# A gated feed-forward behind a chunked scan, one core: seven block products of eight for half of the tiles of blocks 2 and 3 too

## The chip, the cores and the metric

One core of a Trainium2 chip runs the whole kernel. The engines are TensorE (PE), VectorE (DVE), ScalarE (ACT), GpSimd (POOL) and SyncE (SP, which here issues most DMAs). Each engine works through its own list of instructions in order and waits on semaphores. The metric is the device time of one execution in microseconds (us).

## The reference

The first part is a linear attention in chunks over x [4, 8, 768, 32] with decay a and B, C of state size 16; its output, as rows of 256 values per token, goes through a gated feed-forward:

```python
attn_out = _attn_ref(x, a, B, C)                       # [4, 8, 768, 32], a scan over the sequence
x = attn_out.transpose(0, 2, 1, 3).reshape(3072, 256)  # tokens x d_model
gate = 1.0 / (1.0 + np.exp(-(x @ w_gate)))             # w_gate, w_val: 256 x 1536
val = x @ w_val
return gate * val @ w_out                              # w_out: 1536 x 256
```

## The kernel before

The sequence is cut into six chunks of 128 positions; with 4 batches a chunk is a block of 512 tokens, and the blocks are numbered 0 to 5. For each block the scan leaves the feed-forward's input, and then come 12 f tiles of 128 columns of w_gate and w_val.

Everything is fp32, and TensorE's operands are split into a high and a low part (xh, xl; the two halves of w; of h). A product of fp32 values is three matmuls: high by high, high by low, low by high. A gate or value tile of one block (`products_of`, L1244) sums over two halves of d_model, so it is 2 x 3 matmuls of 128x512. ACT takes the sigmoid out of the PSUM bank (L1184), DVE multiplies by the value bank (L1205), ACT writes the high part of h (L1209) and POOL or DVE the low part (L1211). The projection by w_out follows when a block's 12 tiles are done: `proj_turned` (L1529) for blocks 1 to 3, two accumulators of 128x512 over 12 tiles of three matmuls each. DVE turns these back into rows (L1536), and SP stores them with 16 DMAs per block (L1543).

Blocks 4 and 5 are worked as one, "joined". A pair of f tiles, a pair of blocks and the two halves of d_model make a product of 2x2 blocks by 2x2 blocks, and that is done with seven block products in place of eight. The seven stationary operands of an f pair are four blocks of w itself or sums of them (`s_block` builds the sums: one add of high and low parts, L1323, four adds of 128x128, L1330, a high part, L1333, a low part, L1335), and the moving operands are inputs or sums of inputs (`x_block`: x-b11, b21, b22, t1 to t4). `group(i)` issues the seven products, 3 matmuls each (L1368), into three PSUM banks a, b and d (`gva`, `gvb`, `gvd`); even i is a gate, odd i the value of the same f pair. `corner(i, n)` takes the four results 11, 22, 21, 12 out: ACT copies one bank (L1401), DVE adds the other (L1403), then a sigmoid (L1406) or a product with the gate (L1410). Each copy or add frees a bank that the next product needs. `h_parts` makes the two parts of h (L1420, L1422), and `out_of` adds its share to the accumulators of the outputs (matmuls of 256 columns, L1455, so that blocks 4 and 5 come out in rows). `stored_rows` and `last_rows` (L1469, L1479, L1481) copy these and store them.

The scan runs beside all this, in pairs of units named chunk_batch (4_0, 4_2, 5_0, 5_2). Its matmuls stand in `block(n)`: block7, for instance, needs the weighted masks m of units 5_0 and 5_1 (`weights`, L777 on DVE), block8 those of 5_2 and 5_3.

The order of the work is a table, ORDER (from L18). Each word of it, such as pe.group3 or dve.corner3_11, sends one step of a named task to an engine; an engine's instructions stand in the order of its words. Where a step may run on two engines, the table's prefix decides. Tiles in SBUF are shared over time by tags ("h0" to "h11", "r0", "ab", ...): a tile that takes a tag over waits for the readers of the one before.

Of the kernel before, what the change touches and what calls it, by code (L numbers as in the profile page):

```python
# [95 lines left out]
pool.value2_6 pe.block6 dve.value2_7 dve.decays5_3 act.value2_7 pool.value2_7 pe.gate2_8 dve.result4_0
act.inner4_2 sp.x5_2 dve.result4_0 pool.before5_0 dve.after4_2 pe.value2_8 dve.after4_2 act.gate2_8
dve.after4_2 dve.after4_2 pool.decays5_2 pe.gate2_9 dve.value2_8 pool.decays5_3 dve.after4_2 act.value2_8
dve.after4_2 pe.value2_9 act.gate2_9 pool.value2_8 dve.weights5_0 sp.p5_2 dve.weights5_0 pe.gate2_10
dve.value2_9 dve.turn5_2 act.value2_9 pe.value2_10 act.gate2_10 pool.value2_9 act.turn5_2 pe.gate2_11  # L100
# [1777 lines left out]
```

## Time and profile before

| | before |
|---|---|
| median of 3 runs (lowest, highest) | 352.55 us (351.44, 353.85) |
| the profiled execution, and its span | 352.14 us, 350.4 us |
| PE, DVE, ACT, POOL busy | 343.4, 231.2, 174.6, 170.9 us |
| DMA, mean over the span | 78 GB/s |

A span runs from the first to the last instruction. Busy times of different engines overlap; which of them sets the end is read from the chain of work. Starts and ends of matmuls are modelled, and the time of an instruction includes what it loses to others once it has begun.

### The profile page before, as it was taken

How to read it: one execution, taken by the hardware profiler on the slowest of the kernel's cores; microseconds unless marked ns; L12 is line 12 of the kernel's file. 1: busy time of each engine (PE TensorE's matmuls, PEld its weight loads, DVE VectorE, ACT ScalarE, POOL GpSimd, SP SyncE). 2: the span in 40 equal slices, each digit the busy share in tenths (PEclk: the TensorE clock that was granted, in tenths of full speed). 3: DMA queues.
4: the chain of work that ended last, by engine and by line, in shares of the span. 5: the costliest groups of instructions: out<-in, count | busy, mean ns of one | idle time of the engine just before them, and what ended most of it. 6: DMA issues, size and time to landing. Idle time of an engine off the chain costs nothing.

```text
span 350.4 us, 8223 instructions
## 1 busy us (share of the span) xinstructions
PE 343.4 (98%) x3306; PEld 275.9 (79%) x3306; DVE 231.2 (66%) x406; ACT 174.6 (50%) x328; POOL 170.9 (49%) x179
## 2 busy tenths in 40 slices
PE   8989999999999999999999999999999999999995
PEld 4568477787788888888878788888888888888884
DVE  7878678777597687684653336357767677574553
ACT  2565874425965531244551235553546574654542
POOL 6536676666779763235646656866001516032100
PEclk9999999999999999999999999999999999999999
DMA  7998974335646635634300011000002000000003
GB/s 172 209 273 221 278 242 124 110 82 88 137 123 141 134 73 112 115 70 91 61 20 4 2 30 32 0 0 2 1 0 59 4 0 2 0 0 2 0 2 120
DMA packets 87419, 27.43 MB, mean 78 GB/s; under 512 B 75670, under 2 KB 80214, under 8 KB 87382
## 3 DMA queue, kind: packets, MB, share of 16 engines
q1 hardware_dynamic: 82806, 26.13, 31.4%
q10 hardware_dynamic: 4576, 0.79, 1.2%
q8 instruction: 26, 0.43, 0.5%
q14 instruction: 11, 0.09, 0.1%
HBM read 23.46 MB, written 3.44 MB: 77 GB/s over the span
## 4 chain that ended last, share of the span: by engine, by line
PE 86%; DMA 2%; DVE 2%; ACT 1%; POOL 1%; SPq 1%; issue 0%; POOLq 0%; DVEq 0%; ACTq 0%
PE pg L1244 16%; PE pv L1244 16%; PE po L1529 14%; PE acc L1455 8%; PE po L1568 7%; PE gva L1368 6%; PE gvb L1368 6%; PE gvd L1368 5%; DMA wr<-in_moe_w_val_dram 2%; PE banks L784 2%; PE banks L768 1%; PE banks L814 1%; PE acce L1449 1%; POOL w L496 1%; PE acc L1449 1%; DVE wr L459 1%
## 5 line engine op out<-in xcount | busy, mean ns | idle before, releaser
L1211 POOL TENSOR_TENSOR h<-g,h 128x512 fp32r<-128x512 f32 x35 | 47.4, 1355 | 34.8 <-ACT h L1209 34.7
L1244 PE MATMUL pg<-xh,w 128*128 128x512 f32 x168 | 59.3, 394 | 0.0
L1244 PE MATMUL pv<-xh,w 128*128 128x512 f32 x168 | 58.9, 391 | 0.1
L1529 PE MATMUL po<-h,w 128*128 128x512 f32 x216 | 51.3, 392 | 0.0
L1529 PEld LDWEIGHTS po<-h,w 128*128 128x128 f32 x216 | 40.2, 188 | 8.6
L1205 DVE TENSOR_TENSOR g<-pv,g 128x512 f32<-128x512 f32 x36 | 24.8, 689 | 33.3 <-PE pv L1244 33.2
L1209 ACT CAST h<-g 128x512 fp32r<-128x512 f32 x34 | 21.1, 620 | 34.9 <-DVE g L1205 33.3
L1244 PEld LDWEIGHTS pg<-xh,w 128*128 128x128 f32 x168 | 31.5, 188 | 7.8 <-DVE h L1201 0.8
L1244 PEld LDWEIGHTS pv<-xh,w 128*128 128x128 f32 x168 | 31.5, 188 | 7.2 <-POOL w L496 0.5
L1244 PE MATMUL pg<-xl,w 128*128 128x512 f32 x84 | 32.7, 390 | 0.0
L1244 PE MATMUL pv<-xl,w 128*128 128x512 f32 x84 | 32.7, 389 | 0.0
L1184 ACT ACTIVATE g<-pg 128x512 f32<-128x512 f32 x44 | 26.3, 598 | 12.5 <-PE pg L1244 12.2
L1455 PEld LDWEIGHTS acc<-w,h 128*128 128x128 f32 x219 | 29.8, 189 | 2.3
L1455 PE MATMUL acc<-w,h 128*128 128x256 f32 x219 | 30.6, 282 | 0.0
L496 POOL TENSOR_TENSOR w<-wr,w 128x512 fp32r<-128x512 f32 x18 | 26.7, 1483 | 7.7 <-ACT w L494 6.8
L574 DVE TENSOR_TENSOR_SCAN ab<-ab,delta 128x512 f32<-128x512 f32 x20 | 26.7, 1353 | 2.8 <-DMA ab<-a_z 2.8
L1422 POOL TENSOR_TENSOR h<-c,h 128x512 fp32r<-128x512 f32 x7 | 11.4, 1645 | 34.9 <-ACT h L1420 34.9
L477 POOL TENSOR_TENSOR wr<-wr 128x512 int32<-128x512 int32 x18 | 19.9, 1113 | 12.5 <-ACT wr L475 7.7
L1568 PE MATMUL po<-wr,h 128*128 128x256 f32 x96 | 23.4, 394 | 0.1
L1420 ACT CAST h<-c 128x512 fp32r<-128x512 f32 x24 | 14.7, 622 | 15.9 <-DVE c L1410 11.8
L1403 DVE TENSOR_TENSOR c<-gva,c 128x512 f32<-128x512 f32 x12 | 8.3, 691 | 21.1 <-PE gva L1368 21.1
L1568 PEld LDWEIGHTS po<-wr,h 128*128 128x128 f32 x96 | 17.6, 188 | 4.3 <-DVE h L1201 0.5
(205 smaller groups left out, 690.1 us busy)
## 6 DMA issues: line engine op xcount, KB each, us to landing
ab<-a_z SPq DMA_DIRECT2D x40, 128.0 KB
wr<-in_moe_w_gate_dram SPq DMA_DIRECT2D x6, 512.0 KB
wr<-in_moe_w_val_dram SPq DMA_DIRECT2D x6, 512.0 KB
wr<-in_moe_w_out_dram SPq DMA_DIRECT2D x6, 512.0 KB
xn<-in_x_dram SPq DMA_DIRECT2D x10, 256.0 KB
out_dram<-o SPq DMA_DIRECT2D x48, 32.0 KB
bn<-in_B_dram SPq DMA_DIRECT2D x10, 128.0 KB
tn<-in_B_dram SPq DMA_DIRECT2D x32, 32.0 KB
```

The lines of the kernel that those rows point to most:

```text
L477: nc.gpsimd.tensor_tensor(out=lw.bitcast(I32), in0=hw.bitcast(I32), in1=lw.bitcast(I32), op=ALU.add)
L496: engines[eng].tensor_tensor(out=lo, in0=lw, in1=hi.bitcast(F32), op=ALU.subtract)
L574: nc.vector.tensor_tensor_scan(out=t.rearrange("p h l -> p (h l)"), data0=t.rearrange("p h l -> p (h l)"), data1=delta.rearrange("p h l -> ...
L1184: nc.scalar.activation(gs[k, f], pm, AF.Sigmoid)
L1205: nc.vector.tensor_tensor(out=g, in0=pm, in1=g, op=ALU.mult)
L1209: copies[eng](hh, g)
L1211: engines[eng].tensor_tensor(out=hl, in0=g, in1=hh.bitcast(F32), op=ALU.subtract)
L1244: nc.tensor.matmul(pm, w[:, part, kt, fs], xx[:, kt], start=(i == 0), stop=(i == 3 * NK - 1))
L1368: nc.tensor.matmul(out, one, two, start=m == 0 and n in (1, 7, 2), stop=m == 2, skip_group_check=True)
L1455: nc.tensor.matmul(mine, one(js), w[:, two, :], start=first and m == 0 and (k == 0 or alone), stop=final and m == 2, skip_group_check=True,)
L1529: nc.tensor.matmul(acc, w[:, part], hs[k, f][:, of_h], start=f == starts[0] and i == 0, stop=f == starts[-1] + size - 1 and i == 2,)
L1568: nc.tensor.matmul(acc[:, :DM], hs[k, f][:, js], whole[NF + f // 2][:, f % 2], start=start, stop=stop, skip_group_check=True,)
```

## The change

Blocks 2 and 3 become a first joined pair for f tiles 6 to 11 (`PAIRS`). Their tiles 0 to 5 are computed as before, and `tiles(k)` ends their plain loop there. The joined work is now 18 groups: q0 to q5 are the three f pairs 6 to 11 of blocks 2 and 3, q6 to q11 the same f pairs of blocks 4 and 5, and q12 to q17 f pairs 0 to 5 of blocks 4 and 5 (`tile_of`, `stage`). The sums of w for the f pairs of q0 to q5 are used again by q6 to q11.

The moving operands of the first stage are the inputs xh, xl of blocks 2 and 3 themselves and four sums made of them (`x_early`, x0t1 to x0t4); those of the second are x1b and x1t. The projection of blocks 2 and 3 is no longer one run of matmuls: `out_early` adds tiles 0 to 5 and `out_of` the shares of the first stage, into four accumulators of 128x512 that stay until `turned_rows` turns and stores both blocks in groups q7 to q9. Sums of w are built in the order 6 to 11, then 0 to 5, in two tiles that are used for all of them (`kept_tile`).

ORDER is laid out anew from the first tiles of block 2 on, about 145 us into the span. Its core in the diff:

```diff
-pe.gate2_4 dve.value2_3 sp.p4_2 dve.after4_0 act.value2_3 dve.after4_0 pe.value2_4 dve.after4_0 sp.x5_0
-pool.value2_11 pe.proj2_0 dve.result4_2 act.inner5_0 pool.before5_2 dve.result4_2 dve.after5_0 pool.xt3_0
+dve.before5_0 pe.outa3_0 pe.outa3_1 dve.result4_2 dve.result4_2 pool.before5_2 dve.weights5_2 pe.outa3_0
+pe.block9 pe.outa2_0 pe.outa2_0 pe.outa2_0 pool.s6 dve.s6 pool.s7 dve.result5_2 dve.result5_2 pe.group0 act.s6
...
     def value(k, f):
-        eng = yield step(("act", "dve"), (ACT_SB, DVE_1), [("proj", k - 1)] + held)
-        hs[k, f] = hp.tile([P, 2, 512], F32R, tag=f"h{f}", name=f"h{k}_{f}")
+        eng = yield step(("act", "dve"), (ACT_SB, DVE_1), [("proj", min(k, 2) - 1)] + held)
+        place_of = f + 6 * (k == NCH - 3)
+        hs[k, f] = hp.tile([P, 2, 512], F32R, tag=f"h{place_of}", name=f"h{k}_{f}")
...
+    def tiles(k):
+        return NF if k < NCH - 4 else NF // 2
...
-    T1, T2 = NCH - 1, NCH - 2
+    PAIRS = ((NCH - 3, NCH - 4), (NCH - 1, NCH - 2))
+    T1, T2 = PAIRS[1]
+    NS, NQ7 = 9, 18
...
+    def tile_of(q):
+        return q + 6 if q < 6 else q if q < NF else q - NF
...
+    def x_early(name):
...
+        eng = yield step(("dve", "pool"), (DVE_MM, 1.29), needs + xs(k2) + (xs(k1) if name != "t3" else []), made, port=True)
+        in0, in1 = first()
+        t = kept_tile(to)
+        engines[eng].tensor_tensor(out=t, in0=in0, in1=in1, op=ALU.subtract)
+        for n, (k, part, m, op) in enumerate(more):
+            eng = yield step(("dve", "pool"), (DVE_MM, 1.29), [], [("t0", name)] if n == len(more) - 1 else [], port=True)
+            engines[eng].tensor_tensor(out=t, in0=t, in1=of(k, part, m), op=op)
+        yield step("act", ACT_SB, home)
+        hi = x_part(0, name, 0)
+        nc.scalar.copy(hi, t)
+        eng = yield step(("dve", "pool"), (DVE_MM, 1.29), [], [("x7", 0, name, 0)], port=True)
+        engines[eng].tensor_tensor(out=x_part(0, name, 1), in0=t, in1=hi.bitcast(F32), op=ALU.subtract)
...
-    def group(i):
+    def group(q):
+        i, at, last = tile_of(q), stage(q), q - 1
...
+    def h_parts(s, n):
...
+        elif s == 4:
+            needs = [("stored", k2)] if m == 3 else [("hused", 2, PLACES[m + 1])]
...
+    def turned_products(block, mt, f, h, first, final):
+        w = wo[f // 2][:, f % 2, :, mt * P : (mt + 1) * P]
+        for m, (one, two) in enumerate(((0, 0), (0, 1), (1, 0))):
+            nc.tensor.matmul(
+                acc_of(block, mt), w[:, one], h[:, two], start=first and m == 0, stop=final and m == 2, skip_group_check=True
+            )
+
+    def out_early(k, mt):
+        fs = [2, 3, 4, 5, 0, 1] if k == PAIRS[0][0] else list(range(6))
+        for f in fs:
...
+            yield step("pe", 3 * 0.227, needs, [("outa", k, mt, f)], port=12)
+            turned_products(k, mt, f, hs[k, f], f == fs[0], False)
...
+    def out_of(s, n):
...
+        if s < 3:
+            for mt in range(2):
+                yield step("pe", 3 * 0.228, [("h7", s, n), ("w", NF + f // 2), ("outa", block, mt, 1)], ([("hused", s, n)] if mt else []) + [("o7", s, n, mt)], port=12)
+                turned_products(block, mt, f, hj[s, n], False, (s, n) == (2, last))
+            return
...
+    def turned_rows(k):
+        last = "21" if k == PAIRS[0][0] else "12"
+        for mt in range(2):
+            yield step("dve", 0.74, [("o7", 2, last, mt), ("done", 5)], [("turned", k, mt)])
...
+            nc.vector.transpose(outs[k].rearrange("p b (m t) -> p t b m", t=2)[:, mt], acc)
+        for b in range(NB):
+            yield step("sp", 4 * 0.47, [], [("stored", k)] if b == NB - 1 else [])
...
+            for q in range(NQ):
+                nc.sync.dma_start(
+                    rows[:, :, 64 * q : 64 * q + 64], outs[k][32 * q : 32 * q + 32, RUN * b : RUN * b + RUN]
+                )
```

Three places of the new order are shown, with the lines of each program as they stand in it; the numbers behind the names are those of the tiles.

PE before, the gate of f tile 6 of block 2 (pg is the gate's bank, w6 the weights of tiles 6 and 7), one tile of one block:

```order
L1244 MATMUL pg2_6_2359<-xh2_1587,w6_598 128x512
L1244 MATMUL pg2_6_2359<-xl2_1588,w6_598 128x512
L1244 MATMUL pg2_6_2359<-xh2_1587,w6_598 128x512 x2
L1244 MATMUL pg2_6_2359<-xl2_1588,w6_598 128x512
L1244 MATMUL pg2_6_2359<-xh2_1587,w6_598 128x512
```

PE now, group q2, gate of tiles 8 and 9 of blocks 2 and 3 (s8 the sums of w, x0t1 to x0t4 sums of inputs, acc the accumulators of the outputs of blocks 2 and 3; of its last product, by xh2 and xl2, the rows are like the first):

```order
L1426 MATMUL gvd_2877<-x0t3_2320,s8_2922 128x512 x3
L1509 MATMUL acc3_0_2579<-h0_11_2994,w15_1399 128x512 x3
L1426 MATMUL gvb_2878<-xh3_2049,w8_634 128x512
L1426 MATMUL gvb_2878<-xl3_2050,w8_634 128x512
L1426 MATMUL gvb_2878<-xh3_2049,w8_634 128x512
L1426 MATMUL gva_2876<-x0t2_2712,s8_2922 128x512 x3
L1426 MATMUL gvd_2877<-x0t4_2834,w8_634 128x512 x3
L1509 MATMUL acc3_1_2708<-h0_11_2994,w15_1399 128x512 x3
L1426 MATMUL gva_2876<-x0t1_2603,s8_2922 128x512 x3
L1509 MATMUL acc2_0_2817<-h0_22_3002,w15_1399 128x512 x3
L1509 MATMUL acc2_2903<-h0_22_3002,w15_1399 128x512 x3
```

Four tiles (two f tiles of two blocks) were 24 matmuls and are seven products of three, and matmuls of the projection stand between them.

DVE from block7 to block8 before (g2_11 is the last value tile of block 2; m5_2 and m5_3 are what block8 waits for; y the scan's output):

```order
L1205 TENSOR_TENSOR g2_11_2605<-pv2_11_2598,g2_11_2605 128x512
L908 TENSOR_TENSOR y4_2_2506<-banks_1179,y4_2_2506 128x2x2x64
L905 TENSOR_TENSOR y4_2_2506<-banks_1179,y4_2_2506 128x2x64
L905 TENSOR_TENSOR y4_2_2506<-local_1271,y4_2_2506 128x2x64
L676 TENSOR_TENSOR ml5_0_2704<-local_1271,mask_102 128x128
L777 TENSOR_TENSOR m5_2_2709<-banks_1179,ab5_2_2058 128x512
L754 SCALAR_TENSOR_TENSOR sm10_2706<-sn8_2319,pp5_0_2356,ml5_0_2704 128x64 x2
L777 TENSOR_TENSOR m5_3_2728<-banks_1179,ab5_3_2085 128x512
```

DVE now, between the same two blocks (g3_5 is the last plain value tile, x0t1 the low part of a sum of inputs):

```order
L1218 TENSOR_TENSOR g3_5_2616<-pv3_5_2609,g3_5_2616 128x512
L1223 CAST h3_5_2620<-g3_5_2616 128x512
L1225 TENSOR_TENSOR h3_4_2622<-g3_4_2601,h3_4_2622 128x512
L1327 TENSOR_TENSOR x0t1_2603<-ctotal_2392,x0t1_2603 128x512
L689 TENSOR_TENSOR ml5_0_2698<-local_1271,mask_102 128x128
L790 TENSOR_TENSOR m5_2_2701<-banks_1179,ab5_2_2058 128x512
L767 SCALAR_TENSOR_TENSOR sm10_2700<-sn8_2335,pp5_0_2380,ml5_0_2698 128x64 x2
L869 TENSOR_TENSOR cd5_0_2724<-bct5_0_2376,pp5_0_2380 128x256
L921 TENSOR_TENSOR y4_2_2521<-banks_1179,y4_2_2521 128x2x2x64
L918 TENSOR_TENSOR y4_2_2521<-banks_1179,y4_2_2521 128x2x64
L918 TENSOR_TENSOR y4_2_2521<-local_1271,y4_2_2521 128x2x64
L790 TENSOR_TENSOR m5_3_2737<-banks_1179,ab5_3_2085 128x512
```

A cast, two low parts and cd5_0 have come in ahead of m5_3, and the y's have moved ahead of it.

DVE at the end before (copies and last sums of the output rows o of blocks 4 and 5):

```order
L1422 TENSOR_TENSOR h5_12_4095<-c10_12_4035,h5_12_4095 128x512
L1410 TENSOR_TENSOR c10_21_4008<-c11_21_4056,c10_21_4008 128x512
L1422 TENSOR_TENSOR h5_21_4117<-c10_21_4008,h5_21_4117 128x512
L1469 COPY o4_1_4155<-acc4_1_3479 128x2x2x128
L1481 TENSOR_TENSOR o5_2_4123<-acc_3460,o5_2_4123 128x2x128
L1481 TENSOR_TENSOR o5_3_4125<-acce_3463,o5_3_4125 128x2x128
```

DVE at the end now:

```order
L1464 TENSOR_TENSOR c2_2917<-c6_2962,c2_2917 128x512
L1492 TENSOR_TENSOR h8_12_4038<-c3_2939,h8_12_4038 128x512
L1492 TENSOR_TENSOR h8_21_4053<-c2_2917,h8_21_4053 128x512
L1585 COPY o4_1_4085<-acc4_1_3473 128x2x2x128
L1585 COPY o5_0_4094<-acc5_0_3392 128x2x2x128
L1597 TENSOR_TENSOR o5_2_4067<-acc5_3417,o5_2_4067 128x2x128
L1597 TENSOR_TENSOR o5_3_4065<-acce_3420,o5_3_4065 128x2x128
```

The copy of o5_0 has moved from ACT to DVE, and the product for corner 21 stands ahead of the low part of h 12. The stores of o4_0, o4_1, o5_0 and o5_2 are issued by ACT now and that of o5_3 by SP; before it was o5_0 and o5_3 by ACT and the other three by SP.

## Rows read from the trace of the kernel before

**Rows 1.** The page: the span, and part 1, busy us by engine.

```profile
span 350.4 us, 8223 instructions
PE 343.4 (98%) x3306; PEld 275.9 (79%) x3306; DVE 231.2 (66%) x406; ACT 174.6 (50%) x328; POOL 170.9 (49%) x179
```

**Rows 2.** The chain in order of time: start us, us, what.

```profile
146.58 1.36 PE pg L1244 x6
...
236.10 1.36 PE pv L1244 x6
...
248.34 0.68 PE gva L1368 x3
...
264.66 0.71 PE acc L1455 x6
```

**Rows 3.** Windows of 10 us: busy us and count by engine, PE clock, DMA.

```profile
100.00:110.00 10.00, 10.00 (x195) 8.11 (x194) 8.12 (x13) 6.44 (x11) 9.16 (x8) 1.00 0.73 163
...
250.00:260.00 10.00, 10.00 (x46) 8.29 (x45) 6.19 (x12) 6.82 (x12) 1.29 (x1) 1.00 0.00 1
```

**Rows 4.** DVE's groups by shape from 145 on: busy, mean ns, idle before.

```profile
L1422 DVE TENSOR_TENSOR h<-c,h 128x512 fp32r<-128x512 f32 x17 | 13.0, 769 | 4.0 <-ACT h L1420 3.9
L1410 DVE TENSOR_TENSOR c<-c,c 128x512 f32<-128x512 f32 x16 | 12.0, 752 | 0.5
L1330 DVE TENSOR_TENSOR sw<-ww 128x128 f32<-128x128 f32 x24 | 8.4, 349 | 1.3 <-POOL ww L1323 1.2
...
L1403 DVE TENSOR_TENSOR c<-gvb,c 128x512 f32<-128x512 f32 x12 | 8.3, 689 | 2.9 <-PE gvb L1368 2.9
...
L908 DVE TENSOR_TENSOR y<-banks,y 128x256 f32<-128x256 f32 x5 | 2.1, 425 | 9.7 <-PE banks L784 4.8 <-PE local L814 3.8 <-ACT y L893 0.7
```

**Rows 5.** The same view of ACT and of POOL.

```profile
L1406 ACT ACTIVATE c<-c 128x512 f32<-128x512 f32 x18 | 11.4, 632 | 7.2 <-DVE c L1403 7.2
...
L1296 POOL TENSOR_TENSOR xt<-t,xt 128x256 fp32r<-128x256 f32 x8 | 5.8, 735 | 4.1 <-ACT xt L1294 4.1
L1335 POOL TENSOR_TENSOR s<-sw,s 128x512 fp32r<-128x512 f32 x4 | 5.2, 1295 | 24.1 <-ACT s L1333 24.1
```

**Rows 6.** Timelines of DVE and POOL from 293 to 297: start us, us, what.

```profile
294.72 1.01 DVE L1422 TENSOR_TENSOR h<-c,h 128x512 fp32r<-128x512 f32 x1
...
293.61 1.57 POOL L1422 TENSOR_TENSOR h<-c,h 128x512 fp32r<-128x512 f32 x1 [0.73 <-ACT h L1420]
```

**Rows 7.** Chain, and timelines of PE and DVE, around block7 and block8.

```profile
182.58 1.36 PE pv L1244 x6
...
185.91 5.74 PE L1529 MATMUL po<-h,w 128*128 128x512 f32 x24
192.00 0.81 PE L784 MATMUL banks<-m,xn 64*32 64x64 f32 x61
...
185.79 0.42 DVE L908 TENSOR_TENSOR y<-banks,y 128x256 f32<-128x256 f32 x1 [1.06 <-PE banks L784]
...
188.46 0.69 DVE L777 TENSOR_TENSOR m<-banks,ab 128x512 f32<-128x512 f32 x1
```

**Rows 8.** SP's timeline over block 3's stores, and a window after them.

```profile
263.41 7.43 SPq L1543 DMA_DIRECT2D out_dram<-o  x16
...
272.00:274.00 2.00, 2.00 (x13) 1.75 (x13) 0.00 (x0) 1.49 (x3) 0.29 (x1) 1.00 0.03 8
```

**Rows 9.** The timeline of the end.

```profile
344.84 0.69 DVE L1469 COPY o<-acc 128x512 f32<-128x512 f32 x1 [0.46 <-PE acc L1455]
345.56 0.61 ACT L1469 COPY o<-acc 128x512 f32<-128x512 f32 x1 [0.80 <-PE acc L1455]
...
345.99 0.43 DVE L1481 TENSOR_TENSOR o<-acc,o 128x256 f32<-128x256 f32 x1 [0.46 <-PE acc L1455]
...
346.35 0.42 DVE L1481 TENSOR_TENSOR o<-acce,o 128x256 f32<-128x256 f32 x1
...
346.80 0.35 ACTq L1483 DMA_DIRECT2D out_dram<-o  x1
```

More of the change, by code (lines that the diff above doesn't have):

```diff
@@ L96 @@
[L96 to L100, printed above, removed]
@@ L161 @@
+dve.rows5_2 dve.rows5_3 sp.rows5_3 act.rows5_2
 """
@@ new lines, in moved, with kept_tile @@
+    def moved(at, name):
+        if at == 0 and name[0] == "b":
+            return [("x", PAIRS[0][int(name == "b22")], i) for i in range(NB)]
+        return [("x7", at, name, late) for late in range(2 if at else 1)]
+    kept_tiles = {}
+    def kept_tile(n):
+        if n not in kept_tiles:
+            tag = ("g", "g", "g", "tn", "xn", "xn", "ab", "ab")[n] if isinstance(n, int) else "ab"
+            pool, bufs = {"g": (wk, 3), "tn": (ld, 1), "xn": (ld, 2), "ab": (ld, NDEC)}[tag]
+            kept_tiles[n] = pool.tile([P, 512], F32, tag=tag, name=f"c{n}", bufs=bufs)
+        return kept_tiles[n]
@@ L1288, in x_block @@
[L1288 to L1296 removed]
+        half = lambda n, part: x_part(1, n, part)[:, late * 2 * P : (late + 1) * 2 * P].rearrange("p (u i l) -> p i u l", u=2, i=2)
@@ L1321, in s_block @@
+        busy = [[x.get(i, (("sums", "s7")[n], last))] for n, x in enumerate(other)]
+        eng = yield step(("pool", "dve"), (1.29, DVE_MM), needs + busy[0], port=True)
         w = wgv[i]
-        ww = ld.tile([P, NK, 2 * P], F32, tag="ab", name=f"ww{i}", bufs=NDEC)
+        ww, t = kept_tile("sum").rearrange("p (k f) -> p k f", k=NK), kept_tile("total").rearrange("p (n f) -> p n f", n=4)
         engines[eng].tensor_tensor(out=ww, in0=w[:, 0].bitcast(F32), in1=w[:, 1].bitcast(F32), op=ALU.add)
-        yield step("dve", 4 * 0.28, [("s7", i - 1)] if i else [], [("sums", i)], port=True)
@@ L1370, in nth @@
-    def nth(i, n):
-        return 7 * (i // 2) + ("11", "22", "21", "12").index(n) + (0 if i % 2 == 0 else 4)
-    def temp(i, n):
-        tag = ("g", "g", "g", "ut", "ut", "tn", "xn", "xn")[nth(i, n) % 8]
-        pool, bufs = {"g": (wk, 3), "ut": (wk, 2), "tn": (ld, 1), "xn": (ld, 2)}[tag]
-        temps[i, n] = pool.tile([P, 512], F32, tag=tag, name=f"c{i}_{n}", bufs=bufs)
-        return temps[i, n]
-    def corner(i, n):
-        gate = i % 2 == 0
-        free = [("free", nth(i, n) - 8)] if nth(i, n) > 7 else [("h", T2 - 1, f) for f in range(NF - 3, NF)]
-        if (i, n) in ((0, "12"), (1, "11")):
-            free += [("x7", k, late) for k in ("b22", "t1", "t2", "t3") for late in range(2)]
+                nc.tensor.matmul(to, one, two, start=m == 0 and n in (1, 7, 2), stop=m == 2, skip_group_check=True)
@@ L1833, in tile_ssd_then_gated_ffn @@
             t += GV0_T / 2
-        for f in range(NF):
+        for f in range(tiles(k)):
             if halved(k, f):
```

417 lines of the change are left out of this document (237 added, 180 removed).

## The prediction

> **What bounds the kernel now.** The page first: TensorE (PE) is busy for 343.4 of a span of 350.4 us [rows 1]. A busy PE can still wait, since ends of matmuls are modelled, so the chain of work in order of time comes next. From 146.58 on it holds nothing but PE, piece after piece without a hole: six matmuls of a gate or value tile take 1.36 us, at the first tile of block 2 as at the last of block 3, and three of a block product take 0.68 (0.69 where the 0.71 of a projection step of 256 columns stand beside them) [rows 2]. [...] A matmul less is then worth 0.227 us, if nothing else comes to end last. The table by stage shows how far the others are from that: VectorE (DVE) and GpSimd (POOL) were at 8.12 and 9.16 of 10 us in an early stage without a hole in PE, and at 6.19 and 1.29 where the block products start [rows 3].
>
> **What is removed.** For f tiles 6 to 11 of blocks 2 and 3, 24 tiles of six matmuls (gate and value) go: 144. Six groups of seven products of three matmuls come: 126. That is 18 fewer, and the first pair of order fences shows one such tile and one such group. The output projection keeps its 144 matmuls of 128x512 for the two blocks, those of h from the six groups written one by one between the products. 18 x 0.227 = 4.08 us. PE's rows differ in nothing else, so a gain above 4.08 has no source, and a gain of nothing needs waits.
>
> **What is added elsewhere.** The price lies on DVE, ScalarE (ACT) and POOL: per pair of groups 28 elementwise instructions of 128x512 instead of 16. The densest stretch is that of the six new groups (I call them q0 to q5), in which the moved inputs of the later twelve groups are made too. PE needs 42 products and 22 steps of output projection there, 64 x 0.68 = 43.5 us.
>
> ACT has 59 instructions there, none above 0.632 [rows 5]: at most 37.3, hidden.
>
> DVE has 21 that read a PSUM bank (0.69), 8 products of two corners (0.752), 7 lower halves of h (0.769), 5 more of 128x512 (0.69), 20 of 128x128 (0.349) and 10 of 256 columns (0.425) [rows 4]: 14.5 + 6.0 + 5.4 + 3.5 + 7.0 + 4.3 = 40.7 us. POOL has 11 of 256 columns (0.735) and 8 of 512 (1.295 when undisturbed) [rows 5]: 18.4. DVE at 40.7 of 43.5 fits as a sum, but each group has four points where PE needs a bank that DVE or ACT must have read, so slack in one group does not help the next. That is the open term: what PE waits there. Its lower end is 0. Its upper end takes a row that shows the two engines in each other's way: a DVE instruction begun at 294.72 took 1.01 instead of 0.69 beside a POOL instruction begun at 293.61, which took 1.57 instead of 1.295 [rows 6]. Instructions of DVE with a PSUM input are not lengthened (0.689 on average), those with two SBUF inputs are, by 0.06 to 0.08 on average [rows 4]. If none of POOL's 18.4 us lay beside DVE work, DVE's 39.6 undisturbed us (41 x 0.69 + 7.0 + 4.3) and POOL's 18.4 would take 58.0, 14.5 more than PE. I take 0.7 us, near the lower end, because the mean rows, which contain that disturbance, still give a sum below PE's, and because the joined stage of before has such meetings without a hole in PE.
>
> [...]
>
> **What is moved.** The scan blocks of the last two chunks (block6 to block9) come closer together, with the new inputs x0t1 to x0t4 made among them. I followed the tightest of them, the second pair of order fences. block8 needs m of unit 5_3 from DVE. Before, that was done at 189.15 and block8 began at 192.00, 6.09 after block7 had ended at 185.91, with 24 matmuls in between [rows 7]; there are 24 now too. Now four more instructions stand ahead of it: the product g of tile 5, which waits for the last value tile just before block7, a cast, and two lower halves, at most 4 x 0.77 = 3.0. Block7 lasts 1.97 (183.94 to 185.91), so these end 1.3 after block7 (-1.97 + 0.25 to the start + 3.0). The series that took 3.36 before, from 185.79 to 189.15, follows, 0.65 of it a wait for ACT that is now covered, plus one more product cd of 0.43: 3.1. That ends 4.4 after block7, 1.7 us before block8. In the same time POOL has three lower halves and a cd, 3 x 1.295 + 0.735 = 4.6. If all of them get ahead of DVE, block8 starts 2.9 late; if they lie beside its PSUM readers, 0. I take 0.5: a third of such meetings would not use up the slack, two thirds would, by 1.4.
>
> **The end.** The third pair of fences. ACT copied o5_0 at 345.56 while DVE was free to begin o5_2 at 345.99 and o5_3 at 346.35, and the last store was issued at 346.80 [rows 9]. Now DVE copies o5_0 as well (0.69, to 346.25), so o5_2 begins 0.26 later and the last store with it: + 0.25.
>
> **Sum.** -4.08 + 0.7 + 0.5 + 0.25 = -2.63. The profiled execution took 352.14 us, its span 350.4; that gives 349.5. The median of the runs shown, 352.55, is 0.41 above it: 349.9.
>
> **Rivals.**
> All of it is kept. For it: the chain shows no hole from 146.58 on, at DVE loads up to 8.12 in 10 us [rows 2, 3]. Against it: 40.7 of 43.5 is more than any stage from 145 on had. Only the end costs: 352.55 - 4.08 + 0.25 = 348.7.
>
> DVE and POOL in turn become the bound in q0 to q5. Place: DVE's add of the second corner, which frees the bank of PE's last product of each group, with the chain add, product, lower half behind it. Price: with a share s of POOL's 18.4 us not beside DVE work, PE waits 39.6 + 18.4 s - 43.5. It takes back the whole gain at s = 0.42, gives 354.0 at s = 0.5, and is slower by over 1% from s = 0.61; at s = 1 it gives 363.2. For it: rows 6, and 11 short POOL instructions that come in q3 to q5 just where DVE has its own. Against it: 14.5 us of DVE's work there reads PSUM and is not lengthened [rows 4]. I call this the slower rival.
>
> A wait for stores. The stores of blocks 2 and 3 are issued together, 32 of them, where each 16 take 7.43 us [rows 8], and ACT's cast of h4_21 waits for them since it writes the tile they read. The second transposes of the two blocks end some 2.4 us after group q8 begins; 32 stores later it is 17.3, and traffic ended within 1.5 to 3 us of the last issue (270.84 against the window from 272) [rows 8]: 18.8 to 20.3. The cast can run when the sum and product ahead of it are done, some 20.5 after q8 begins (q8 and q9 are 14 products of 0.69 and 8 steps of 0.71 [rows 2], 15.3; five more products, 3.45; then 1.7). It hides, barely; 2 us later than that would hold ACT's whole queue, the gate sums of q10 behind it, and give 351.9.
>
> That the change does not take the matmuls away can be excluded: the counts above are those of the built programs.
>
> **How the numbers follow.** About 1% is what a measurement of this kernel can tell: below 349.0 is faster, above 356.1 slower. Forecast, waits of 0.3 to 2.2 us: 0.50, with 349.0 to 350.9. All kept: 0.26, 348.5 to 349.0. DVE and POOL in turn, waits above 2.2: 0.18, of which a third beyond 356.1. Stores: 0.04, and 0.02 for what I don't see. Faster is the second case and the edge of the first, 0.30; slower is 0.06 + 0.02; the rest is 0.62. The range reaches from 348.0, all kept less the scatter of the runs, to 352.7, waits of 4 us, where half of the third case is left out.
>
> **What would show it.** The block products of q0 to q5 should show PE pieces of 0.68 with holes of 0.1 to 0.5 us at a few last products of a group; a hole ahead of block8 below 1 us; DVE's mean for lower halves in 146 to 275 at 0.75 to 0.85. Means above 1.0 there, and one hole per group, are the slower rival; a hole in q10 ended by ACT's cast is the stores; no hole at all is the case where all is kept. I am wrong if the start of q0, or PE's rate in it, differs from what the matmul count gives.

## The result and the profile after

| | before | changed |
|---|---|---|
| median of 6 runs each (lowest, highest) | 352.83 us (351.44, 353.85) | 349.12 us (347.58, 351.22) |
| ratio to before, 95% interval | | 0.9898 (0.9861 to 0.9935) |
| the profiled execution's span | 350.4 us | 349.4 us |

The time went down by 1.0%. The forecast was 349.9 us, with a range of 348.0 to 352.7; the rival "all of it is kept" had said 348.7.

The profiled execution of the changed kernel is the slowest of its six. The chain of waits shows that this lies ahead of everything that was changed: its first tile of block 2, answering to [rows 2], starts 3.29 us later (149.87 against 146.58), after a part in which both programs issue the same instructions in the same order. So the two traces are compared from that tile on.

The changed kernel's page, span and busy times, answering to [rows 1]:

```profile
span 349.4 us, 8257 instructions
PE 339.2 (97%) x3288; PEld 271.9 (78%) x3288; DVE 253.7 (73%) x441; ACT 181.5 (52%) x349; POOL 177.4 (51%) x177
```

PE has 18 matmuls fewer and DVE 22.5 us more. The chain of the changed kernel in order of time (start us, us, what), answering to [rows 2]:

```profile
149.87 1.36 PE pg L1261 x6
...
204.03 0.68 PE gva L1426 x3
...
247.55 0.68 PE gva L1426 x3
...
291.02 0.69 DVE c L1457
292.22 1.78 DVE c L1464
294.67 0.96 PE gvb L1426 x3
```

The pieces of a product take 0.68 from q0 (204.03) through q6 (247.55) and on, as before the change, with nothing of another engine between them. There is one place where the chain leaves PE, at 291: two DVE instructions, one of them of 1.78 us, and PE starts late at 294.67. That is between groups q11 and q12, not in q0 to q5.

The last matmuls of both kernels, from the timelines of the end (start us, us, what), the first of before and the second of the changed kernel:

```profile
345.72 0.52 PE L1455 MATMUL acce<-w,h 128*128 128x256 f32 x3
```

```profile
344.80 0.52 PE L1550 MATMUL acce<-w,h 128*128 128x256 f32 x3
```

From the first tile of block 2 to the end of these it is 346.24 - 146.58 = 199.66 us before and 345.32 - 149.87 = 195.45 now: 4.21 less, in one trace each. From there to the end of the span it is 4.16 and 4.08.

DVE and POOL in q0 to q5, a window from q0's start to q6's (busy us and count of PE, PEld, DVE, ACT, POOL; PE clock):

```profile
203.87:247.40 43.53, 43.53 (x194) 36.04 (x193) 36.18 (x67) 29.14 (x58) 18.07 (x17) 1.00 0.00 1
```

The stretch is 43.53 us long, the 43.5 of the matmul count. DVE is busy for 36.18 of it and not for 40.7, POOL for 18.07.

### The profile page after: what moved, and what is told of

Same layout as the page of the kernel before. It is cut to its first block, busy times and chain, and to the rows that moved or that the text cites. A ratio compares the mean times of both kernels' runs of the same rounds, so it can differ in the third digit from the quotient of the medians.

```text
span 349.4 us, 8257 instructions
## 1 busy us (share of the span) xinstructions
PE 339.2 (97%) x3288; PEld 271.9 (78%) x3288; DVE 253.7 (73%) x441; ACT 181.5 (52%) x349; POOL 177.4 (51%) x177
## 4 chain that ended last, share of the span: by engine, by line
PE 83%; DVE 3%; POOL 2%; DMA 2%; ACT 1%; issue 1%; SPq 1%; DVEq 0%; ACTq 0%; POOLq 0%
PE pg L1261 11%; PE pv L1261 10%; PE acc L1509 10%; PE gvb L1426 9%; PE gva L1426 9%; PE acc L1550 7%; PE gvd L1426 7%; PE po L1691 7%; PE po L1652 5%; DMA wr<-in_moe_w_val_dram 2%; PE banks L797 2%; PE banks L781 1%; POOL w L509 1%; PE banks L827 1%; PE acc L1544 1%
## 5 line engine op out<-in xcount | busy, mean ns | idle before, releaser
L1261 PE MATMUL pg<-xh,w 128*128 128x512 f32 x120 | 42.7, 396 | 0.8 <-DVE g L1218 0.8
L1261 PE MATMUL pv<-xh,w 128*128 128x512 f32 x120 | 42.1, 392 | 0.1
L1225 POOL TENSOR_TENSOR h<-g,h 128x512 fp32r<-128x512 f32 x19 | 27.5, 1448 | 23.5 <-ACT h L1223 20.4
L1509 PE MATMUL acc<-h,w 128*128 128x512 f32 x144 | 36.9, 392 | 0.0
L1492 POOL TENSOR_TENSOR h<-c,h 128x512 fp32r<-128x512 f32 x18 | 24.5, 1371 | 24.2 <-ACT h L1490 23.5
L1509 PEld LDWEIGHTS acc<-h,w 128*128 128x128 f32 x144 | 26.8, 188 | 5.7
L1261 PEld LDWEIGHTS pg<-xh,w 128*128 128x128 f32 x120 | 22.5, 188 | 7.1 <-DVE g L1218 1.2
L490 POOL TENSOR_TENSOR wr<-wr 128x512 int32<-128x512 int32 x18 | 20.0, 1116 | 13.8 <-ACT wr L488 6.5
L1261 PEld LDWEIGHTS pv<-xh,w 128*128 128x128 f32 x120 | 22.4, 188 | 5.3 <-POOL w L509 0.6
L1457 DVE TENSOR_TENSOR c<-gva,c 128x512 f32<-128x512 f32 x18 | 12.4, 691 | 17.3 <-PE gva L1426 16.4
L1261 PE MATMUL pg<-xl,w 128*128 128x512 f32 x60 | 23.4, 390 | 0.0
L1261 PE MATMUL pv<-xl,w 128*128 128x512 f32 x60 | 23.4, 389 | 0.0
```

The costliest lines, as they stand in the source:

```text
L490: nc.gpsimd.tensor_tensor(out=lw.bitcast(I32), in0=hw.bitcast(I32), in1=lw.bitcast(I32), op=ALU.add)
L1225: engines[eng].tensor_tensor(out=hl, in0=g, in1=hh.bitcast(F32), op=ALU.subtract)
L1261: nc.tensor.matmul(pm, w[:, part, kt, fs], xx[:, kt], start=(i == 0), stop=(i == 3 * NK - 1))
L1492: engines[eng].tensor_tensor(out=hj[s, n][:, 1], in0=g, in1=hj[s, n][:, 0].bitcast(F32), op=ALU.subtract)
L1509: nc.tensor.matmul(acc_of(block, mt), w[:, one], h[:, two], start=first and m == 0, stop=final and m == 2, skip_group_check=True)
```

## The experiments

All are the changed kernel with the edit shown. Since what an edit does is small beside the scatter of the early stage, two lengths of each trace are compared: from the first matmul of the scan's block4, 7.7 us ahead of the first tile of block 2, to the first matmul of q0 ("to q0"), and from there to the end of the last matmul ("from q0").

| run | ratio to before (95%) | to q0 | from q0 |
|---|---|---|---|
| the change | 0.9898 (0.9861 to 0.9935) | 61.88 | 141.45 |
| e1_matmuls_back | 0.9995 (0.9977 to 1.0013) | 61.87 | 145.54 |
| e2_dve_twice | 0.9987 (0.9973 to 1.0002) | 61.88 | 145.16 |
| e3_dve_thrice | 1.0194 (1.0163 to 1.0225) | 61.87 | 150.87 |
| e10_in_idle | 0.9905 (0.9881 to 0.9928) | 61.87 | 141.91 |
| e11_no_idle | 0.9960 (0.9936 to 0.9983) | 61.87 | 143.90 |
| e5_pool_twice | 1.0181 (1.0138 to 1.0225) | 61.88 | 150.65 |
| e4_product_later | 0.9874 (0.9839 to 0.9910) | 61.94 | 141.12 |
| e12_two_moves | 0.9872 (0.9848 to 0.9897) | 61.88 | 141.12 |
| e6_before_block8 | 0.9947 (0.9922 to 0.9971) | 64.31 | 141.45 |
| e9_before_m5_3 | 0.9965 (0.9946 to 0.9984) | 65.47 | 141.45 |
| e8_stores_later | 0.9948 (0.9927 to 0.9970) | 61.95 | 143.43 |
| e7_end | 0.9883 (0.9856 to 0.9909) | 61.94 | 141.45 |

### Is it the matmuls? (e1_matmuls_back)

```diff
-            for m, (one, two) in enumerate(((wh, xh), (wh, xl), (wl, xh))):
-                nc.tensor.matmul(to, one, two, ...)
+            for again in range(2 if q < 6 and n == 7 else 1):
+                for m, (one, two) in enumerate(((wh, xh), (wh, xl), (wl, xh))):
+                    nc.tensor.matmul(to, one, two, ...)
```

> The second product of each of the six new groups (its three matmuls of 128x512 into bank d) is issued twice, the second time from a fresh start of the bank, so that 18 matmuls come back into the stretch from which 18 went. I compare the time from the start of the first gate tile of block 2 to the end of the last matmul: 199.66 us before, 195.45 with the change. Theory (TensorE's list at full rate sets the end, 0.227 us a matmul): 195.45 + 4.08 = 199.5 us, all of it between the starts of q0 and q6 (43.5 becomes 47.6), and in the medians a ratio to the kernel before of 0.9898 + 4.08/352.8 = 1.001. Rival (the saving was not the matmuls but the new order, and TensorE only looks busy while DVE's list sets the pace of the new groups): less than half of it comes back, at most 2 us, a ratio below 0.996.

Measured: from q0 it is 145.54, 4.09 more, and the ratio is 0.9995. So 18 matmuls cost 18 x 0.227 here, and what they save is on the path in full.

### How near was DVE to being the bound? (e2_dve_twice, e3_dve_thrice)

```diff
+        for again in range(2 if s < 3 and eng == "dve" else 1):    # e3: 3
             engines[eng].tensor_tensor(out=hj[s, n][:, 1], in0=g, in1=hj[s, n][:, 0].bitcast(F32), op=ALU.subtract)
```

> Each of the seven lower halves of h that DVE makes in the new groups q0 to q5 is made twice: seven more instructions of 128x512 with two SBUF inputs, 7 x 0.7 to 0.83 = 4.9 to 5.8 us. DVE was busy for 35.8 of the 43.0 us from 204 to 247, so it comes to 40.7 to 41.6: the load that the prediction had worked out (40.7). Theory (the sum below PE's 43.5 is enough, slack of one group helps the next): the stretch from q0 to q6 stays at 43.5 within 0.2 us, the time within 0.3 us of the changed kernel's. Rival (each group has four points where a bank must be read, so slack of one group does not help the next): one hole per group that has a doubled half, 0.2 to 0.7 each, 1 to 3 us in all.

> The same seven lower halves three times: fourteen more instructions, 9.8 to 11.6 us, so DVE has 45.6 to 47.4 us in a stretch of 43.5. Theory (the sum counts): the stretch grows by what exceeds 43.5, 2.1 to 3.9 us, with PE holes ended by DVE's adds. Rival 1 (points within groups): 4 us or more. Rival 2 (DVE's work can slip behind q5 into the later groups, where DVE was busy for 31.7 of 44): below 1.5 us.

Measured: seven more lower halves cost 3.71 us, fourteen 9.42. The theory that the sum counts falls twice, and 3.71 is more than the 1 to 3 us of the rival of the first; each of the second seven costs 0.82 us, more than it lasts undisturbed. PE's timeline of e2_dve_twice (start us, us, what, and in brackets the idle time ahead and what ended it) shows the waits, here the three longest:

```profile
223.13 0.50 PE L1426 MATMUL gva<-xh,s 128*128 128x512 f32 x1 [0.78 <-DVE c L1457]
...
237.00 0.96 PE L1426 MATMUL gva<-x0t,s 128*128 128x512 f32 x3 [0.62 <-ACT c L1455]
...
250.80 0.96 PE L1426 MATMUL gvb<-x1b,w 128*128 128x512 f32 x3 [0.71 <-DVE c L1448]
```

Each is a product that needs a bank: freed late by DVE's add (L1457), by DVE's product of corner 12 (L1448), or by ACT's copy (L1455), which itself waits for a lower half of DVE, because that reads the buffer the copy writes. From q0's start to q6's, DVE was busy for only 40.97 of 46.22 us (a window as before):

```profile
201.67:247.89 46.22, 44.69 (x194) 35.65 (x192) 40.97 (x73) 29.14 (x58) 18.14 (x17) 1.00 0.00 1
```

Of the 3.71, 2.7 lie in this stretch and the rest in q6.

### The amount, or the place? (e10_in_idle, e11_no_idle)

```diff
+        for again in range(2 if (s, n, eng) == (0, "21", "dve") else 1):             # e10
+        for again in range(4 if (name, late) == ("b21", 1) else 1):                  # e10, lower half in x_block
+        ) * (2 if i == 9 else 1):                                                    # e10, the four adds of s_block
...
+        for again in range(2 if eng == "dve" and (s, n) in ((1, "22"), (1, "21"), (1, "12"), (2, "11")) else 1):  # e11
```

> DVE gets 2.4 us more in q0 to q5 at places where it waited for PE with the change: the four adds of 128x128 of the sums of f tiles 9 twice (idle 1.06 behind them, 4 x 0.20 more), the lower half of corner 21 of the first f pair twice (idle 0.79, 0.60 more), the lower half of x1b21 of the late chunks four times (idle 1.45, 3 x 0.34 more). DVE is then busy for 38.6 of 43.5. Theory (what counts is the slack up to the next bank that PE waits for, not the sum): no new hole, the time from q0's start to the end of the last matmul stays at 141.45 within 0.1 us. Rival (the doubled lower halves cost what they did because DVE was full as a whole, 3.7 us for 4.9): 1.2 to 1.8 us longer.

> The same 2.4 us more for DVE in q0 to q5, but where it had little or no idle time before the next bank: four lower halves of h (corners 22, 21 and 12 of the second f pair, corner 11 of the third) are made twice, 4 x 0.60. Theory (slack up to the next bank): holes of 0.4 to 1.0 us at the three places that showed them when all seven were doubled (the first at the end of q3 or in q4, one in q5, one at the first product of q6 into the bank of corner 12), 1.5 to 2.4 us together. Rival (the sum counts, 38.6 of 43.5): no hole, 141.45 from q0's start to the end of the last matmul.

Measured: 0.46 us in the one, 2.45 in the other. The windows from q0 to q6, of e10_in_idle and then of e11_no_idle:

```profile
202.10:246.10 44.00, 43.83 (x194) 35.98 (x193) 40.22 (x75) 29.30 (x58) 18.07 (x17) 1.00 0.00 1
```

```profile
202.70:247.70 45.00, 44.33 (x194) 35.83 (x193) 38.14 (x70) 29.06 (x58) 18.04 (x17) 1.00 0.00 1
```

Both edits add 2.4 us of undisturbed work, and the kernel in which DVE is busy longer, 40.22 us, waits less than the one with 38.14. So it is the slack up to the next bank that counts. The expectation for e10 was nevertheless missed by one hole of 0.44, behind the doubled lower half. Timelines of DVE and of POOL in e10_in_idle there:

```profile
218.59 2.39 DVE L1494 TENSOR_TENSOR h<-c,h 128x512 fp32r<-128x512 f32 x2
```

```profile
218.82 1.61 POOL L1384 TENSOR_TENSOR csum<-w 128x512 f32<-128x512 f32 x1 [1.02 <-DVE ctotal L1390]
```

Two lower halves take 1.29 undisturbed; these took 2.39, and they end 0.55 after POOL's instruction has ended (218.82 + 1.61 = 220.43). Since one alone takes 0.68 to 0.69 in this trace, most of the second one's work came after POOL's end; that is an estimate from these times.

### What does POOL's work cost DVE? (e5_pool_twice)

```diff
+        for again in range(2 if s < 3 and eng == "pool" else 1):      # lower halves of h
+        for again in range(2 if eng == "pool" else 1):                # lower halves in x_block
+        for again in range(2 if 8 <= i and eng == "pool" else 1):     # s_block: the first add, the lower half
```

> POOL's work in q0 to q5 is made twice where an instruction can be repeated (lower halves of h, of the sums of w and of the new inputs, and the first adds of the sums of w): about 14 instructions, 13.7 us more, so POOL has some 31.8 of 43.5 us in place of 18.1; DVE's list is as it was. Theory (a meeting with POOL lengthens a DVE instruction with two SBUF inputs now and then, and the slack of 7.7 us takes it): DVE's means for products and lower halves rise to 0.85 to 1.0, no hole or holes below 0.5 us in all. Rival (DVE and POOL in turn, the slower rival of the prediction: POOL's whole time counts to a large share s): DVE's 21 us without a PSUM input and POOL's 31.8 take turns; the sum is 35.8 + 31.8 s against 43.5, over it from s = 0.24, and at s = 0.5 PE waits 8 us.

Measured: 9.20 us more from q0. The theory of small holes falls. The window from q0's start to q6's, and DVE's groups by shape in it (busy, mean ns of one, idle before):

```profile
202.54:249.73 47.19, 45.12 (x193) 35.49 (x192) 42.62 (x66) 29.10 (x58) 31.87 (x29) 1.00 0.00 1
```

```profile
L1467 DVE TENSOR_TENSOR c<-c,c 128x512 f32<-128x512 f32 x7 | 7.7, 1107 | 0.2
...
L1496 DVE TENSOR_TENSOR h<-c,h 128x512 fp32r<-128x512 f32 x7 | 6.9, 984 | 0.0
...
L1460 DVE TENSOR_TENSOR c<-gva,c 128x512 f32<-128x512 f32 x6 | 4.1, 685 | 1.7 <-PE gva L1429 1.7
```

The same groups of the changed kernel in its window:

```profile
L1492 DVE TENSOR_TENSOR h<-c,h 128x512 fp32r<-128x512 f32 x7 | 5.8, 828 | 0.0
L1464 DVE TENSOR_TENSOR c<-c,c 128x512 f32<-128x512 f32 x8 | 5.7, 723 | 0.2
...
L1457 DVE TENSOR_TENSOR c<-gva,c 128x512 f32<-128x512 f32 x6 | 4.1, 690 | 3.1 <-PE gva L1426 3.1
```

DVE's products went from 723 to 1107 ns and its lower halves from 828 to 984; its adds out of PSUM stayed at 690 and 685. With the same list of its own but for one instruction at the edge (66 records for 67), DVE is busy 42.62 - 36.18 = 6.4 us longer for 13.8 us more of POOL: for these the share s of the prediction is 0.47. By the prediction's formula that is still below 43.5, so no wait; PE waited all the same. 47.19 - 43.53 = 3.7 us of waits lie in the stretch itself, most of them ended by DVE. The larger part, 5.5, came behind it: mostly POOL's own lateness, and 1.6 of it a lower granted clock after these waits (last section). Timelines of POOL, ACT and PE in e5_pool_twice:

```profile
256.63 5.74 POOL L1496 TENSOR_TENSOR h<-c,h 128x512 fp32r<-128x512 f32 x4
...
262.40 0.59 ACT L1458 COPY c<-gvb 128x512 f32<-128x512 f32 x1 [2.15 <-POOL h L1496]
...
263.04 0.96 PE L1429 MATMUL gvb<-x1t,s 128*128 128x512 f32 x3 [1.77 <-ACT c L1458]
```

ACT's copy waits for the lower half on POOL that still reads its buffer, and PE for that copy. So the run shows both causes, in nearly equal parts (3.7 us in the stretch, some 3.9 behind it), and does not separate them further.

### The one hole (e4_product_later, e12_two_moves)

Timelines of PE, DVE and POOL of the changed kernel around it:

```profile
293.61 0.84 PE L1426 MATMUL gvd<-x1t,s 128*128 128x512 f32 x3
294.67 0.96 PE L1426 MATMUL gvb<-x1b,w 128*128 128x512 f32 x3 [0.21 <-DVE c L1448]
...
291.62 2.38 DVE L1464 TENSOR_TENSOR c<-c,c 128x512 f32<-128x512 f32 x2
293.93 0.68 DVE L1448 TENSOR_TENSOR c<-gvb,c 128x512 f32<-128x512 f32 x1
...
291.94 1.52 POOL L1492 TENSOR_TENSOR h<-c,h 128x512 fp32r<-128x512 f32 x1 [0.73 <-ACT h L1490]
```

It is the meeting of [rows 6] again: two products of DVE, 1.29 undisturbed, take 2.38 beside a lower half on POOL, and the product of corner 12, which frees a bank, stands behind them. PE starts 0.38 late and the piece loses 0.11 more. The edits of the order:

```diff
-dve.corner11_22 act.part5_22 pe.group11 pe.group12 act.corner12_11 dve.corner11_12 act.part5_12
+pe.group11 pe.group12 act.corner12_11 dve.corner11_12 dve.corner11_22 act.part5_22 act.part5_12
...
-dve.part5_12 pool.part5_11 pe.group12 pe.group12 dve.corner12_11     (e12 alone)
+pool.part5_11 pe.group12 pe.group12 dve.corner12_11 dve.part5_12
```

> In the order, DVE's product of corner 22 of group q11 and ACT's cast of it stand after DVE's product of corner 12 and after ACT's first copy of q12. Nothing else is changed. The trace of the changed kernel has one hole in PE after q0, at 294.3: 0.38 us, and 0.11 more in the piece behind it, where the first use of a bank in q12 waits for DVE's product of corner 12 of q11; that stood behind a product that took 1.78 us in place of 0.69, from 292.22, beside a lower half of POOL from 291.94 to 293.46. Theory (that one meeting makes the hole): the hole is gone, 195.45 becomes 195.0 +- 0.1 us. Rival (the stall only moves, to the cast of corner 22 and ACT's queue behind it): another hole of 0.2 to 0.6 us in q12, and the time stays at 195.3 to 195.6.

> The product of corner 22 of q11 after that of corner 12, as before, and besides DVE's lower half of corner 12 behind its first add of q12. With the first move alone the hole of 0.49 went, and 0.33 of it was won from q0's start to the last matmul (141.45 became 141.12); the rest stood as 0.08 and 0.12 behind 294.3, where that lower half took 1.37 in place of 0.69 ahead of the add. Theory: 140.95 +- 0.05, all of the hole won. Rival (the lower half, now later, holds something else): 141.1 or more. In the medians no more than 0.15% against the changed kernel.

Measured: both kernels take 141.12 from q0, 0.33 less, and the hole is gone. The theory of the second one, that the remaining 0.16 was DVE's long lower half, falls. Timelines of PEld and ACT in e12_two_moves show what is left:

```profile
294.51 0.53 PEld L1426 LDWEIGHTS gva<-x1t,s 128*128 128x128 f32 x3 [0.34 <-ACT c L1455]
...
293.88 0.59 ACT L1455 COPY c<-gva 128x512 f32<-128x512 f32 x1 [0.41 <-POOL h L1492]
```

ACT's copy waits for a lower half on POOL, and PE for the copy. Both kernels come out ahead of the changed one in the trace, and e12_two_moves has the lowest median measured, 348.84 us; in the medians 0.33 us is within the intervals.

### The slack ahead of block8 (e6_before_block8, e9_before_m5_3)

```diff
+        for again in range(5 if (k, f) == (3, 4) else 1):      # e6: lower half of h of tile 4, block 3
...
+        for again in range(5 if name == "t1" else 1):          # e9: lower half of x0t1
```

> DVE makes the lower half of h of tile 4 of block 3, which stands four instructions after the start of block7 and ahead of m of unit 5_3, five times: four more instructions, 4 x 0.69 = 2.7 us (more beside POOL). With the change the product m5_3 ended at 194.39 and block8's matmuls that need it began at 195.96, 1.57 later, with no hole in PE. Theory (slack 1.57, to be used up): PE waits ahead of block8 for 2.7 - 1.57 = 1.1 us, 1.0 to 1.6 with meetings, and the whole gets longer by the same. Rival 1 (the real slack is less since block8 also waits for something that lies further behind on DVE): 2 us or more. Rival 2 (DVE's waits for ACT and POOL between them take the delay in): below 0.5 us.

> The delay ahead of m of unit 5_3 again, now by an instruction that no matmul waits for before q0: DVE's lower half of x0t1, which stands just ahead of the series that ends in m5_3, is made five times. With the change DVE's instructions of this form start 0.60 apart when they follow each other undisturbed, so four more are 2.4 us (up to 4 with meetings with POOL). Theory (m5_3 ended at 194.39, the matmuls of block8 that read it began at 195.96, so 1.57 of slack): block8 starts 0.8 to 1.5 us later, with the hole at block8 and not before it; no other change up to q0 beyond what block9 and x0t4 lose by it, 0.5 at most. Rival (the wait for h3_4 in the run before was the whole effect, and m5_3 has more slack than 1.57): no hole ahead of block8.

Measured: 2.43 and 3.59 us more up to q0. In e6 most of the wait came before block8, since the projection reads the very tile that was delayed; so it says little of m5_3. PE's timeline of e6_before_block8:

```profile
192.64 3.51 PE L1510 MATMUL acc<-h,w 128*128 128x512 f32 x14 [1.25 <-DVE h L1226]
```

In e9 it is m5_3. Timelines of PE and DVE in e9_before_m5_3:

```profile
195.02 0.28 PE L827 MATMUL banks<-cd,sn 32*64 32x64 f32 x3 [2.04 <-DVE m L790]
...
187.04 4.69 DVE L1328 TENSOR_TENSOR x0t<-ctotal,x0t 128x512 fp32r<-128x512 f32 x5
...
193.97 0.68 DVE L790 TENSOR_TENSOR m<-banks,ab 128x512 f32<-128x512 f32 x1
```

Put on one clock by the start of block4 (2.64 earlier in this run), m5_3 starts 2.90 later than with the change and block8 2.11 later: the slack is 0.79, not 1.57, and the hole 2.11 where the theory had 0.8 to 1.5. Block8's first matmuls do not read m, but the wait stands at the first of them, and block8 starts 0.37 after m5_3's end (194.65 to 195.02).

Then block9 and q0 lost 1.48 more, where the theory allowed 0.5. Windows of 1 us of e9_before_m5_3 (the clock is the third column from the end):

```profile
194.00:195.00 1.00, 0.00 (x0) 0.00 (x0) 1.00 (x3) 0.24 (x1) 0.68 (x1) 1.00 0.00 0
195.00:196.00 1.00, 0.98 (x84) 0.92 (x91) 1.00 (x1) 0.00 (x0) 1.00 (x2) 0.86 0.00 0
196.00:197.00 1.00, 1.00 (x48) 0.83 (x36) 0.59 (x3) 0.00 (x0) 1.00 (x1) 0.50 0.05 16
...
199.00:200.00 1.00, 1.00 (x5) 0.77 (x5) 0.12 (x1) 0.62 (x1) 1.00 (x2) 0.93 0.00 0
200.00:201.00 1.00, 1.00 (x7) 0.79 (x5) 1.00 (x2) 0.00 (x0) 0.45 (x1) 1.00 0.06 16
```

After the wait of 2.04 us the granted clock falls to 0.50 in the windows from 196 to 199, and is back at 1.00 from 200 on. The windows at 197 and 198 hold 3 and 4 matmuls and that at 200 holds 7; that is where the 1.48 went.

### The stores and the end (e8_stores_later, e7_end)

```diff
-            for q in range(NQ):
+            for q in [*range(NQ)] * (2 if k == 3 and b < 2 else 1):      # e8, turned_rows
...
-pe.out8_12 act.rows4_0 dve.rows4_1 act.rows4_1 pe.out8_21 dve.rows5_0 act.rows5_0 pe.out8_21
-dve.rows5_2 dve.rows5_3 sp.rows5_3 act.rows5_2
+pe.out8_12 sp.rows4_0 dve.rows4_1 sp.rows4_1 pe.out8_21 act.rows5_0 act.rows5_0 pe.out8_21
+dve.rows5_2 sp.rows5_2 dve.rows5_3 act.rows5_3
```

> The first eight of the 32 stores of blocks 2 and 3 are issued twice (the same rows to the same place), so the stores of block 2 end 8 x 0.508 = 4.1 us later. With the change the 32 took 16.25 us from 264.49, traffic ended between 281 and 282, and ACT's cast of h4_21, which writes the tile that they read, ran at 282.64. Theory (a margin of about 1 us, then ACT's queue is held): the cast runs at about 285.5 to 286, 3 us late, with the gate sums of q10 behind it, and PE gets a hole of 1 to 3 us in q10 or q11; the time grows by that. Rival (the stores are hidden anyway, since q10's gate banks do not need the casts behind it in time): no new hole, within 0.3 us of the changed kernel.

> The end as it was before the change: ACT copies the last rows of o5_0 and issues its store and that of o5_3, SP the stores of o4_0, o4_1 and o5_2. From the end of the last matmul to the end of the span it was 4.16 us before (346.24 to 350.4) and 4.08 with the change (345.32 to 349.4). Theory of the prediction (DVE's copy puts o5_2 and the last store off by 0.25): 0.25 us less, 3.8. Rival (the last store was issued 0.14 later after the last matmul with the change, and from that issue to the end it took 3.38 by SP against 3.60 by ACT, so the two ends are worth the same): 4.0 to 4.2, no difference that the medians can show.

Measured for e8: 1.98 us more, as the theory said. SP, ACT and PE of e8_stores_later:

```profile
262.10 19.93 SPq L1569 DMA_DIRECT2D out_dram<-o  x40
...
283.46 0.62 ACT L1490 CAST h<-c 128x512 fp32r<-128x512 f32 x1 [3.66 <-DMA out_dram<-o]
...
286.10 0.96 PE L1426 MATMUL gva<-x1b,w 128*128 128x512 f32 x3 [1.69 <-ACT c L1444]
```

ACT's cast waits 3.66 us for the stores, the last sigmoid of q10 stands behind it, and PE waits for that. The changed kernel itself, ACT and SP:

```profile
282.64 0.62 ACT L1490 CAST h<-c 128x512 fp32r<-128x512 f32 x1 [0.45 <-DVE c L1464]
...
264.49 16.25 SPq L1569 DMA_DIRECT2D out_dram<-o  x32
```

There the cast waits for DVE. In e8 it ran 283.46 - 282.03 = 1.43 after the last issue; 1.43 after 280.74 is 282.17, so the margin was about 0.5 us.

Measured for e7: from the last matmul to the end of the span 4.11 us against 4.08 (spans are read to 0.1 us), and no difference in the medians. The rival holds.

## Why the prediction was right, point by point

**PE's list at full rate bounds the kernel.** Right: no hole from 149.87 to 294, six matmuls of 128x512 in 1.36 us (0.227 each), the clock at 1.00 in the windows over this length, and e1 gives 18 matmuls a price of 4.09.

**-4.08 for the matmuls.** Right. That a gain above 4.08 has no source was wrong: from block 2 on the trace lost 4.21 although it has a hole of 0.49, so 0.6 more went. With e1, which has as many matmuls as before, it is again 0.6 (61.87 + 145.54 - 0.49 against 207.53 from block4 to the last matmul). Of that, the chain of before shows three pieces of block products that take 0.80 to 0.82 in place of 0.69 to 0.71, 0.35 together, and one run of 256-column matmuls that takes 0.20 longer than the changed kernel's runs of the same length. First two of the four of before (the others are at 314.25 and 329.69), then one of the changed kernel:

```profile
265.37 0.80 PE gvb L1368 x3
...
340.31 2.35 PE acc L1455 x18
```

```profile
339.58 2.15 PE acc L1550 x18
```

So the kernel before lost some time within PE's pieces, where the text saw no loss. The rest, below 0.1, is open; that PE's list has 79 changes between matmuls of 512 and of 256 columns in place of 95 may be part of it (behind a run of 256 columns a piece takes 0.69 at 266.62 of the changed kernel, elsewhere 0.68), which no run sets apart.

**+0.7 for waits in q0 to q5.** Measured: 0. The step that failed is the sum of DVE's time, 40.7 us where DVE was busy for 36.18. A part of it is the list: of the ten instructions of 256 columns that the text counts, four came after q6 had begun (from 248.34). The durations of what lies in the stretch add up to 39.4. And DVE does not take that long, as its timeline in group q1 shows:

```profile
215.02 0.69 DVE L1457 TENSOR_TENSOR c<-gvd,c 128x512 f32<-128x512 f32 x1 [0.62 <-PE gvd L1426]
215.63 0.69 DVE L1457 TENSOR_TENSOR c<-gvb,c 128x512 f32<-128x512 f32 x1
216.24 0.68 DVE L1492 TENSOR_TENSOR h<-c,h 128x512 fp32r<-128x512 f32 x1
216.83 1.29 DVE L1464 TENSOR_TENSOR c<-c,c 128x512 f32<-128x512 f32 x2
218.04 0.69 DVE L1448 TENSOR_TENSOR c<-gvb,c 128x512 f32<-128x512 f32 x1
```

Instructions of 0.69 start 0.60 apart: the next one begins while the last 0.08 to 0.09 of the one before still counts. The stretch has 40 such hand-overs, and they are the 3.2 us between 39.4 and 36.18. The second half of the step, that 40.7 would fit with 0.7 of waits, was wrong too, in the other direction: with DVE busy for 40.97 us in the stretch PE waits 3.7 (e2). The text's own warning, that slack in one group does not help the next, is what e10 and e11 show; it was not given its weight. Two errors cancelled, which was luck. By the sign that the text itself gives, no hole at all in q0 to q5 is its rival "all of it is kept", and that rival describes the stretch better than the forecast does.

**The slower rival, DVE and POOL in turn.** Its mechanism is there: s is about a quarter in the changed kernel, since its 36.18 contain 4.2 us by which instructions with two SBUF inputs are longer than undisturbed (groups by shape, against 0.685, 0.285 and 0.415 for 512, 128 and 256 columns), for 18.07 of POOL; and 0.47 for the extra of e5. Its price was mis-sized: it let DVE and POOL fill all of PE's 43.5 before PE waits, and its 39.6 undisturbed is too long, by the hand-overs and by adds of 128x128 taken at 0.349 that take 0.28 alone. The kernel is much closer to that edge than the break-even of 0.42 says, and e5 ended 1.8% slower than before. What one meeting costs can be read off: a DVE instruction of 128x512 with two SBUF inputs, caught beside POOL, ended 0.54 to 0.55 after POOL's: in [rows 6] (295.18 and 295.73), at q11 (293.46 and 294.00), at x0t1 (190.91 and 191.46) and in e10 (220.43 and 220.98). In [rows 6] POOL's had 0.46 left when DVE's began at 294.72, and 0.46 + 0.55 is the 1.01 seen.

**+0.5 ahead of block8.** Measured: 0 (from block7 to q0 the changed kernel's chain holds PE alone). The time of DVE's list was well estimated: m5_3 ended 4.5 us after block7 (194.39 against 189.88) where the text had 4.4, although the product g, one of its "four more", stands in the list of before too. The estimated slack of 1.7 was 0.79, because the wait stands at block8's first matmul and not at the first that reads m; it sufficed, since only one meeting with POOL, that of x0t1's lower half (1.78 us from 189.68), came in the way.

**+0.25 at the end.** Measured: 0. The last store is issued 0.70 after the last matmul in place of 0.56 [rows 9], so half of the 0.25 is there; but it is SP's, and from its issue to the end of the span it is 3.38 in place of 3.60 after ACT's. The step looked at DVE's queue and not at who issues the last store.

**The stores.** Right: no wait, with 0.5 us to spare, and eight more stores, 3.7 us, cost 1.98 by ACT's queue (e8).

**What was not in the sum.** The hole of 0.49 at q11, by the mechanism of [rows 6], outside the stretch in which it was looked for.

The sum as it should stand: -4.08 - 0.6 + 0.49 = -4.2, against -2.63 in the text. On the medians the change took off 1.02%, 3.6 us of 352.83, between the two; its interval, 2.3 to 4.9 us, contains both, so it is the traces that decide. Of the text's three additions, 1.45 together, none was there. By the traces the text's sum is 1.6 us short; that the median lies only 0.8 from its 349.9 is luck.

## What to carry to other kernels

Price an engine's list by the distance from start to start where its instructions follow each other, not by their durations (0.60 against 0.69 us for DVE's of 128x512 here); then look at each point where the bounding engine needs a result, and at the idle time of the other engine just ahead of it. That engine was busy for 83% of the stretch here and hid all of it, and seven more instructions cost 3.7 us; four instructions' worth cost 0.46 or 2.45 by where it stood. A meeting of DVE and POOL mattered here where a freed bank or buffer stood behind it (the hole of 0.49 at q11, gone in e4), so move the instruction that frees one ahead of those that can be held up.
